# Three MoE-and-dense layers on one core: single tokens' units spread through the mixed steps, narrowing at fixed places, remainders moved

## The chip, the cores and the metric

The kernel runs on one core of a Trainium2 chip. The metric is the device time of one execution in microseconds (us); the median of three runs is compared. TensorE (PE, with its weight loads PEld), VectorE (DVE), ScalarE (ACT), GpSimd (POOL) and SyncE (SP, which here only issues DMAs) each run their own instructions in order and wait for one another by semaphores.

## The reference, cut to what matters

```python
attn = softmax(mask(scale * q @ k.T)) @ v             # 4 batches x 8 heads x 576 tokens
x = attn as 2304 tokens x 512
P = sinkhorn(exp(x @ w_gate))                          # 2304 x 8, eight rounds
out = sum over e of P[:, e] * (relu(x @ w1[e]) @ w2[e])    # 8 experts, 512 -> 1024 -> 512
r = relu(out @ w_in); result = (r * r) @ w_out         # 512 -> 2048 -> 512
```

All in float32; `w_in` and `w_out` arrive as 64-bit floats.

## The kernel before, in words

After the attention (up to about 98 us) the two layers run as 80 *steps*. Each step takes 256 hidden columns, that is one first product and one second product. Steps 0 to 31 do the MoE layer for tokens 0 to 1023 (the *pair*, two halves of 512) and for 256 *single* tokens (1024 to 1279). Steps 32 to 63 do it again for tokens 1280 to 2303, without singles. Steps 64 to 71 and 72 to 79 do the dense layer for the same two groups.

The products of a pair use seven instead of eight block products. Every operand stands as a rounded part and a remainder (`hi`, `lo`), so a block product takes three matmuls per 128 rows. ACT makes a rounded part, DVE the remainder (source minus rounded part). `store` keeps finished weights in DRAM for steps 32 to 63.

A step is a list of *units* on PE, counted from 0. A unit of the pair, or one of the two single units `w0` and `w1` of the second product, is six 512-column matmuls; `us`, the single tokens' first product, is 24 matmuls of 256 columns. `run(u)` runs a unit and then whatever was registered for this place by `after(k, f)`, "k units from now", which becomes the order on ACT, DVE, POOL and SP. Functions registered earlier stand first.

- **Steps 3 to 19 and 65 to 70 ("plain").** Eighteen units: u1 to u4 (0 to 3); a second-product unit ahead of each of u5 (5), u6 (7) and u7 (9); five more (10 to 14); w0, w1, us. In step 20 all of the second product stands ahead of u1. Each second-product unit takes one of three PSUM banks (`mm`) in turn, and DVE adds it to the accumulator (L841 or L845) before the bank is used again.
- **Steps 21 to 31 ("mixed with singles").** The second product too uses seven products (`l2_mixed`, v1 to v7), accumulated by two L925 each. All eight banks are dealt out, and the single units share one (`spare`). `out_mixed` makes four blocks r1, r3, r4, r2; `mix` (L702) combines them with four subtractions on POOL into `t1` to `t4`; ACT rounds them (L670) and DVE makes their remainders (L673). They are used by v5 (t1), v6 (t2), v7 (t3) and v4 (t4) of the next step.
- **Steps 33 to 63 and 73 to 79** are mixed without singles: 14 units.

`prep_w` makes the next weights in the same step: sums on POOL (L190 to L195), rounding on ACT (L172), remainders `blkl`, `suml`, `w2l`, `mixl` on DVE (L176), all at fixed places `at`.

*Narrowing* turns `w_in` and `w_out` into float32 in 32 pieces of 128x512. `narrow` has four parts for a piece: a 512 KB load into an `xb` buffer (SP, L282); first pass (DVE, L289 and L293); second pass (L297, L300); third pass (L304, L307, L311) and a 256 KB store to `w32` (SP, L312). `narrow_on` does the next part, and `done` counts them. In steps 3 to 19 it is called behind units 3, 6, 9 and 12, and once more right after a store, so that the next load follows it at once. By this rule three of every four pieces have their first pass three units behind their load. `settled` finishes a piece that is under way at steps 30, 62 and 70. Steps 52 to 61 and 65 to 68 call it by the table `stages`.

Of the kernel before, what the change touches and what calls it, by code (L numbers as in the profile page):

```python
# [49 lines left out]
def tile_kernel(ctx: ExitStack, tc: tile.TileContext, a):  # L50
# [113 lines left out]
    def prep_w(i, layers=(1, 2)):  # L164
# [21 lines left out]
        elif 1 in layers and n < len(steps):  # L186
# [18 lines left out]
                    load_w(2 * NS1 if n + 1 == NS1 else n + 1, 0)  # L205
                keep("blk")

            at = (4, 5, 6, 8) if n == NS1 else (2, 5, 10, 14) if n < NS1 else (2, 5, 8, 11)
            spread = n > first[2] + 1
            if spread:  # L210
                at = (6, 7, 14, 16)
# [15 lines left out]
        elif i >= 0:  # L227
# [20 lines left out]
                tt(out=r[:, 1, 0], in0=r[:, 1, 0], in1=r[:, 0, 0], op=ALU.subtract)  # L248

            if TURN <= i < NS1:  # L250
                at = (7, 8, 9, 9, 13, 15)
            elif moe:
                at = (0, 0, 0, 1, 9, 11) if i == 0 else (8, 10, 11, 12, 16, 17) if i == 1 else (1, 3, 6, 7, 13, 15)
            else:
                at = (11, 13, 14, 14, 20, 22) if late else (14, 15, 16, 16, 21, 22) if n == first[2] + 2 else (12, 13, 14, 14, 19, 20)
# [395 lines left out]
    def l1_pair(i):  # L651
# [24 lines left out]
        def out_mixed(fc, t, src, k):  # L676
# [18 lines left out]
            if (fc, t) == (0, 0):  # L695
                operand("11", g, k + 1, k + 2)
            elif (fc, t) == (1, 1):
                operand("22", g, *((5, 6) if i + 1 in first else (3, 4)))
            elif (fc, t) == (1, 0):
                operand("21", g, k + 1, k + 2 if moe else k + 3)  # L700
            else:
                sub = lambda o, x, y: nc.gpsimd.tensor_tensor(out=o, in0=x, in1=y, op=ALU.subtract)  # L702

                def mix():
                    sub(r1, r4, r1)
                    sub(r5, r2, r1)
                    sub(r4, r2, r4)
                    sub(r3, r3, r5)

                after(2, mix)  # L710
                operand("t1", r1, 3, 4)
                operand("t2", r5, 4, 5)
                operand("t3", r4, 5, 7)
                operand("t4", r3, 6, 8)

        def out(fc, t, src, k):
            if mixed(i):
# [232 lines left out]
    with tc.manual_schedule():  # L950
# [231 lines left out]
        for i in range(len(steps) + 1):  # L1182
# [23 lines left out]
            if mixed(i - 1):  # L1206
# [9 lines left out]
                    names = "u1 v1 u2 v2 u3 u4 v6 u5 v5 u6 u7 v7 v3 v4"  # L1216
                else:
                    names = "u1 v1 u2 v2 u3 v6 u4 v5 u5 v7 u6 v3 u7 v4"
                if l1s and i < NS1:
                    names += " w0 w1 us"  # L1220
                order = [(u | v)[n] for n in names.split()]
                l2, l2s, l1s, ahead = [], [], [], []
            elif i == TURN:
# [19 lines left out]
            if i == NS1 + 4:  # L1243
                y0 = two(xb()) + two(xb())
                raw = two(raw1.rearrange("p b c -> p (b c)").bitcast(F32R))
                splits.append(blocks_of(1, y_dram[:, :, :2 * T], y0 + raw))
            if i == 2 * NS1 + 1:
                y1 = two(mix32) + tuple(post[0].tile([128, T], F32, tag="pp", name="pp", bufs=3) for _ in range(2))
                splits.append(blocks_of(2, y_dram[:, :, PAIRS[1]:], y1 + two(mixes[0][0]) + two(xb().bitcast(F32R))))
                apart[:] = xb(), post[0].tile([128, T], F32, tag="pp", name="pp", bufs=3)  # L1250
            if SCALED <= i < TURN - 1:
                split_on(0, 8, 9)
            elif NS1 + 4 <= i < 2 * NS1 - 4:
# [6 lines left out]
                    after(8 + 2 * k, f)  # L1260
            stages = {}
            if 2 * NS1 - 12 <= i <= 2 * NS1 - 3:
                stages = ({8: 3, 9: 0}, {8: 1}, {8: 2})[(i - 2 * NS1 + 12) % 3]
            elif 2 * NS1 < i <= 2 * NS1 + 4:
                stages = {1: 0, 4: 1, 9: 2, 17: 3}
            early = (2, 15, 16, 17) if i == SCALED - 1 else (3, 6, 9, 12) if SCALED <= i < TURN else ()
            for k, u in enumerate(order):
                run(u)
                if i < SCALED:
                    next(sink, None)  # L1270
                if stages and done[0] % 4 == stages.get(k):
                    narrow_on()
                if k in early:
                    narrow_on()
                    if done[0] % 4 == 0:
                        narrow_on()
        settle()

# [85 lines left out]
```

## Time and profile before

| | us |
|---|---|
| median of 3 runs | 2034.26 (2031.69 to 2038.37) |
| the profiled execution | 2036.71 |
| its span, first to last instruction | 2034.9 |
| PE busy | 1922.1 (94%) |
| DVE busy | 1676.5 (82%) |
| ACT, POOL busy | 793.0 (39%), 684.8 (34%) |
| mean granted TensorE clock | 0.985 of 2.4 GHz |

A sum made from the trace is compared with the profiled execution's 2036.71. Matmul ends are modelled in the trace, so that "busy" for PE is near, not at, its peak; its idle times and the starts of its matmuls are what to read.

### The profile page before, as it was taken

The numbers are of one execution on the slowest core, as the hardware profiler recorded it, in microseconds if no ns is written. First come the engines' busy times: TensorE is split into PE (matmuls) and PEld (weight loads), VectorE is DVE, ScalarE is ACT, GpSimd is POOL, SyncE is SP. The second block draws the span as 40 slices with busy tenths as digits, with TensorE's granted clock in tenths as the row PEclk, the third lists the DMA queues.
The fourth block names the chain that finished last, engine by engine and source line by source line (L and its number), as shares of the span: only waits on it lengthen the run. The fifth ranks groups of instructions, "written<-read, shape, count | busy, mean of one in ns | idle before, by whom it ended". The sixth has DMA issues, their size and how long they took to land.

```text
span 2034.9 us, 28281 instructions
## 1 busy us (share of the span) xinstructions
PE 1922.1 (94%) x10343; PEld 1576.3 (77%) x10343; DVE 1676.5 (82%) x2468; ACT 793.0 (39%) x1310; POOL 684.8 (34%) x584
## 2 busy tenths in 40 slices
PE   8998899898999899999999999999999999999999
PEld 6677777687777777777788888888888777788887
DVE  7786777676767689999968998998999989985797
ACT  6743232232233344343433333333333344452543
POOL 3523233132132155555513423433323244240331
PEclk9999999898999999999999999999999999999999
DMA  8675676575666545564796766766666687779762
GB/s 299 237 266 208 207 251 219 207 258 191 238 224 237 188 180 182 184 217 180 274 387 244 268 245 262 268 247 255 246 230 237 248 326 279 258 275 383 267 230 80
DMA packets 162554, 492.75 MB, mean 242 GB/s; under 512 B 16928, under 2 KB 32176, under 8 KB 162416
## 3 DMA queue, kind: packets, MB, share of 16 engines
q1 hardware_dynamic: 162416, 490.96, 66.2%
q8 instruction: 81, 1.33, 0.3%
q14 instruction: 57, 0.47, 0.1%
HBM read 282.15 MB, written 208.74 MB: 241 GB/s over the span
## 4 chain that ended last, share of the span: by engine, by line
PE 68%; DVE 20%; DMA 6%; issue 2%; ACT 2%; POOL 1%; SPq 0%; DVEq 0%; POOLq 0%; ACTq 0%
PE pt L591 12%; PE mm L815 12%; PE mm L911 12%; PE s L591 9%; PE xt L591 7%; PE mm L772 5%; DMA xb<-in_w_out 4%; PE xt L911 4%; PE s L911 4%; DVE acc L925 3%; DVE acc L841 2%; DVE g L673 2%; DMA xb<-in_w_in 2%; DVE suml L176 1%; DVE s L751 1%
## 5 line engine op out<-in xcount | busy, mean ns | idle before, releaser
L815 PE MATMUL mm<-w2h,g 128*128 128x512 f32 x928 | 300.0, 405 | 38.5 <-DVE acc L841 38.1
L702 POOL TENSOR_TENSOR r<-mix,r 128x512 f32<-128x512 f32 x51 | 67.2, 1318 | 575.9 <-DVE mix L691 480.1
L673 DVE TENSOR_TENSOR g<-r,g 128x512 fp32r<-128x512 f32 x204 | 207.1, 1019 | 46.7 <-ACT g L670 45.0
L815 PEld LDWEIGHTS mm<-w2h,g 128*128 128x128 f32 x928 | 177.8, 195 | 82.6 <-DVE acc L841 44.8
L670 ACT CAST g<-r 128x512 fp32r<-128x512 f32 x204 | 126.6, 621 | 240.5 <-PE mm L911 113.6
L925 DVE TENSOR_TENSOR acc<-mm,acc 128x512 f32<-128x512 f32 x298 | 191.7, 681 | 12.8 <-PE mm L911 12.8
L815 PE MATMUL mm<-w2l,g 128*128 128x512 f32 x464 | 185.8, 400 | 0.0
L841 DVE SCALAR_TENSOR_TENSOR acc<-mm,ptile,acc 128x512 f32<-128x512 f32 x194 | 141.1, 745 | 38.9 <-PE mm L815 38.6
L190 POOL TENSOR_TENSOR sums<-raw 128x256 f32<-128x256 f32 x40 | 37.0, 924 | 370.3 <-DVE suml L176 322.9
L815 PE MATMUL mm<-w2h,sg 128*128 128x512 f32 x320 | 106.5, 415 | 32.5 <-DVE acc L841 29.1
L670 ACT CAST g<-mix 128x512 fp32r<-128x512 f32 x153 | 94.8, 620 | 86.4 <-POOL mix L702 76.9
L772 PE MATMUL mm<-xs,blkh 128*128 128x256 f32 x624 | 116.5, 287 | 12.2 <-DVE acc L841 10.2
L911 PE MATMUL mm<-g,w2h 128*128 128x512 f32 x408 | 126.3, 391 | 1.0 <-ACT s L915 1.0
L631 ACT ACTIVATE sg<-mm 128x512 fp32r<-128x512 f32 (+1 forms) x33 | 18.9, 573 | 275.3 <-PE mm L772 253.6
L591 PE MATMUL xt<-x_hi,sumh 128*128 128x512 f32 x316 | 123.8, 392 | 2.2 <-DVE s L742 2.2
L591 PE MATMUL pt<-x_hi,sumh 128*128 128x512 f32 x316 | 123.9, 392 | 2.0 <-ACT s L737 2.0
L911 PE MATMUL mm<-g,mixh 128*128 128x512 f32 x408 | 125.7, 389 | 0.0
L591 PE MATMUL s<-x_hi,blkh 128*128 128x512 f32 x316 | 123.5, 391 | 1.1 <-ACT pt L725 1.1
L591 PE MATMUL pt<-x_lo,sumh 128*128 128x512 f32 x316 | 123.4, 391 | 0.0
L591 PE MATMUL pt<-x_hi,suml 128*128 128x512 f32 x316 | 123.3, 390 | 0.0
L591 PE MATMUL s<-x_lo,blkh 128*128 128x512 f32 x316 | 123.1, 390 | 0.0
L591 PE MATMUL s<-x_hi,blkl 128*128 128x512 f32 x316 | 123.1, 390 | 0.0
(264 smaller groups left out, 5083.3 us busy)
## 6 DMA issues: line engine op xcount, KB each, us to landing
raw<-in_w SPq DMA_DIRECT2D x61, 512.0 KB, 4.2
blkh<-w_blkh SPq DMA_DIRECT2D x41, 512.0 KB, 3.7
blkl<-w_blkl SPq DMA_DIRECT2D x41, 512.0 KB, 4.6
sumh<-w_sumh SPq DMA_DIRECT2D x41, 512.0 KB, 5.2
suml<-w_suml SPq DMA_DIRECT2D x41, 512.0 KB, 6.1
w_blkh<-blkh SPq DMA_DIRECT2D x40, 512.0 KB, 5.1
w_blkl<-blkl SPq DMA_DIRECT2D x40, 512.0 KB, 6.1
w_sumh<-sumh SPq DMA_DIRECT2D x40, 512.0 KB, 5.6
```

Source lines behind the costliest of these rows:

```text
L176: nc.vector.tensor_tensor(out=w[1], in0=src, in1=w[0].bitcast(F32), op=ALU.subtract)
L190: tt(out=c(sums, 0), in0=c(raw1, 2), in1=c(raw1, 3), op=ALU.add)
L591: nc.tensor.matmul(ps, w[:, c], z[:, x, j], start=start and k == 0, stop=stop and k == 5, skip_group_check=True)
L670: after(k, lambda: nc.scalar.copy(b[:, 0], src))
L673: lambda: nc.vector.tensor_tensor(out=b[:, 1], in0=src, in1=b[:, 0].bitcast(F32), op=ALU.subtract),
L702: sub = lambda o, x, y: nc.gpsimd.tensor_tensor(out=o, in0=x, in1=y, op=ALU.subtract)
L751: after(0, lambda: nc.vector.tensor_tensor(out=made["s2"], in0=bank_c, in1=made["s2"], op=ALU.add))
L772: nc.tensor.matmul(ps, w[:, c], z[:, kc], start=k == 0, stop=k == len(terms) - 1)
L815: nc.tensor.matmul(ps, g[:, c0 * 128:c0 * 128 + 128], wt[:, fc], start=k == 0, stop=k == 3 * FC - 1)
L841: nc.vector.scalar_tensor_tensor(out=dst, in0=ps, scalar=p, in1=dst, op0=ALU.mult, op1=ALU.add)
L911: nc.tensor.matmul(ps, w[wt][:, c], z[:, g], start=start and k == 0, stop=stop and k == 2, skip_group_check=True)
L925: nc.vector.tensor_tensor(out=o, in0=ps, in1=o, op=ALU.add)
```

## The change

It does five things. In steps 21 to 31 w0, w1 and us no longer stand together at the end: w0 stands behind v2, w1 behind v6 (in step 31 too), us stays last. In steps 20 to 31 the remainders of t1 to t4 are registered later: 7, 6, 9 and 11 units behind u7 instead of 4, 5, 7 and 8; `suml` goes from place 14 to 12 in steps 21 to 30 and the rounding of `mix` from 13 to 14. In steps 3 to 19 the narrowing is called at places that depend on the step's remainder by three, so that every first pass but that of step 3 stands seven units behind its load; the last piece's third pass goes from step 30 to step 20. Step 61 starts no piece any more, so that nothing is left to settle at step 62. The five last pieces, one more than before, are narrowed in steps 64 to 69, each loaded behind unit 8 and narrowed behind units 2, 4 and 6 of the next step.

```diff
-            at = (4, 5, 6, 8) if n == NS1 else (2, 5, 10, 14) if n < NS1 else (2, 5, 8, 11)
+            at = (4, 5, 6, 8) if n == NS1 else (2, 5, 10, 12) if TURN + 1 < n < NS1 else (2, 5, 10, 14) if n < NS1 else (2, 5, 8, 11)
...
             if TURN <= i < NS1:
-                at = (7, 8, 9, 9, 13, 15)
+                at = (7, 8, 9, 9, 14, 15)
...
-                operand("t1", r1, 3, 4)
-                operand("t2", r5, 4, 5)
-                operand("t3", r4, 5, 7)
-                operand("t4", r3, 6, 8)
+                a, b, c, d = (4, 5, 7, 8) if i >= NS1 else (7, 6, 9, 11)
+                operand("t1", r1, 3, a)
+                operand("t2", r5, 4, b)
+                operand("t3", r4, 5, c)
+                operand("t4", r3, 6, d)
...
-                if l1s and i < NS1:
-                    names += " w0 w1 us"
+                if i == first[1] - 1:
+                    names = "u1 v1 u2 v2 w0 u3 u4 v6 w1 u5 v5 u6 u7 v7 v3 v4 us"
+                elif i < NS1:
+                    names = "u1 v1 u2 v2 w0 u3 v6 w1 u4 v5 u5 v7 u6 v3 u7 v4 us"
...
+            if i == 2 * NS1:
+                apart[:] = xb(), post[0].tile([128, T], F32, tag="pp", name="pp", bufs=3)
             if i == 2 * NS1 + 1:
...
-                apart[:] = xb(), post[0].tile([128, T], F32, tag="pp", name="pp", bufs=3)
...
-                stages = ({8: 3, 9: 0}, {8: 1}, {8: 2})[(i - 2 * NS1 + 12) % 3]
-            elif 2 * NS1 < i <= 2 * NS1 + 4:
-                stages = {1: 0, 4: 1, 9: 2, 17: 3}
-            early = (2, 15, 16, 17) if i == SCALED - 1 else (3, 6, 9, 12) if SCALED <= i < TURN else ()
+                stages = ({8: 3, 9: 0} if i < 2 * NS1 - 3 else {8: 3}, {8: 1}, {8: 2})[(i - 2 * NS1 + 12) % 3]
+            elif 2 * NS1 <= i <= 2 * NS1 + 5:
+                stages = {2: 1, 4: 2, 6: 3, 8: 0}
+            early = ()
+            if i == SCALED - 1:
+                early = (2, 15, 16, 17)
+            elif SCALED <= i <= TURN:
+                early = ((1, 3, 5, 12), (1, 3, 10, 12), (1, 8, 10, 12) if i < TURN else (1,))[i % 3]
...
-                    if done[0] % 4 == 0:
+                    if done[0] % 4 == 0 and i < TURN:
                         narrow_on()
```

The change adds no instruction; it moves them. Three places show it. In the changed kernel the lines from 711 on have other numbers: L841 is L842, L742 is L743, L751 is L752, L925 is L926.

First, DVE in the middle of step 13 (remainder 1): before, with the third pass of a piece, whose end releases the next load, close ahead of the next first pass.

```order
L304 TENSOR_SCALAR xb<-xb 128x512
L307 SCALAR_TENSOR_TENSOR xb<-xb 128x512
L311 TENSOR_TENSOR xb<-xb 128x512
L841 SCALAR_TENSOR_TENSOR acc_1873<-mm,ptile,acc_1873 128x4x128
L624 SCALAR_TENSOR_TENSOR g_1876<-s_152,g_1876 128x512
L624 SCALAR_TENSOR_TENSOR g_1876<-pt,g_1876 128x512
L329 TENSOR_TENSOR pp<-z_1887,pp 128x512
L751 TENSOR_TENSOR s_151<-xt,s_151 128x512
L289 TENSOR_SCALAR xb<-xb 128x512
L293 SCALAR_TENSOR_TENSOR xb<-xb 128x512
```

The same stretch of step 13 on DVE now.

```order
L176 TENSOR_TENSOR blkl_142<-raw_111,blkh_141 128x1024
L842 SCALAR_TENSOR_TENSOR acc_1873<-mm,ptile,acc_1873 128x4x128
L743 TENSOR_TENSOR s_152<-xt,s_152 128x512
L842 SCALAR_TENSOR_TENSOR acc_1873<-mm,ptile,acc_1873 128x4x128
L624 SCALAR_TENSOR_TENSOR g_1876<-s_152,g_1876 128x512
L624 SCALAR_TENSOR_TENSOR g_1876<-pt,g_1876 128x512
L329 TENSOR_TENSOR pp<-z_1887,pp 128x512
L752 TENSOR_TENSOR s_151<-xt,s_151 128x512
L842 SCALAR_TENSOR_TENSOR acc_1873<-mm,ptile,acc_1873 128x4x128
L289 TENSOR_SCALAR xb<-xb 128x512
L293 SCALAR_TENSOR_TENSOR xb<-xb 128x512
```

The third pass has gone ahead of `blkl` to unit 3, and the first pass stands one unit further back, behind unit 10.

Second, SP's queue in step 12 (remainder 0): before, the narrowing's store and load (L312, L282) stand behind the second raw weights' load and the two stores of `pp`.

```order
L158 DMA raw_111<-in_w 128x1024
L139 DMA w_blkh<-blkh_147 128x1024
L139 DMA w_blkl<-blkl_148 128x1024
L158 DMA raw_113<-in_w 128x1024
L331 DMA b_dram_99<-pp 128x512 x2
L312 DMA w_96<-xb 128x512
L282 DMA xb<-in_w_out 128x1024
L139 DMA w_sumh<-sumh_149 128x1024
```

The same place of SP's queue now.

```order
L158 DMA raw_111<-in_w 128x1024
L139 DMA w_blkh<-blkh_147 128x1024
L139 DMA w_blkl<-blkl_148 128x1024
L312 DMA w_96<-xb 128x512
L282 DMA xb<-in_w_out 128x1024
L158 DMA raw_113<-in_w 128x1024
L331 DMA b_dram_99<-pp 128x512 x2
L139 DMA w_sumh<-sumh_149 128x1024
```

The pair of L312 and L282 now follows the two `blk` stores at once, and the second raw load waits behind it.

Third, DVE at the change from one mixed step to the next: before, with the singles' accumulations of w0 and w1 (L841) around `suml`, then `mixl` and the remainders of t1 and t2 (`g<-r`).

```order
L925 TENSOR_TENSOR acc_1873<-xt,acc_1873 128x512
L841 SCALAR_TENSOR_TENSOR acc_1874<-mm,ptile,acc_1874 128x512
L176 TENSOR_TENSOR suml_144<-sums,sumh_143 128x1024
L841 SCALAR_TENSOR_TENSOR acc_1874<-mm,ptile,acc_1874 128x512
L176 TENSOR_TENSOR mixl_1881<-raw_113,mixh_1880 128x1024
L673 TENSOR_TENSOR g_1875<-r_6184,g_1875 128x512
L673 TENSOR_TENSOR g_1876<-r_6186,g_1876 128x512
L624 SCALAR_TENSOR_TENSOR sg<-mm,sg 128x512
L673 TENSOR_TENSOR g_1876<-mix_1878,g_1876 128x512 x2
L925 TENSOR_TENSOR acc_1873<-mm,acc_1873 128x512 x2
```

DVE from the end of a mixed step into the next one now.

```order
L926 TENSOR_TENSOR acc_1873<-xt,acc_1873 128x512
L624 SCALAR_TENSOR_TENSOR sg<-mm,sg 128x512
L673 TENSOR_TENSOR g_1876<-r_6190,g_1876 128x512
L926 TENSOR_TENSOR acc_1873<-mm,acc_1873 128x512 x2
L842 SCALAR_TENSOR_TENSOR acc_1874<-mm,ptile,acc_1874 128x512
L673 TENSOR_TENSOR g_1875<-r_6188,g_1875 128x512
L176 TENSOR_TENSOR blkl_142<-raw_111,blkh_141 128x1024
L691 SCALAR_TENSOR_TENSOR r_6188<-s,pp 128x512
L673 TENSOR_TENSOR g_1876<-mix_1878,g_1876 128x512
L926 TENSOR_TENSOR acc_1873<-s,acc_1873 128x512
L926 TENSOR_TENSOR acc_1873<-xt,acc_1873 128x512
L842 SCALAR_TENSOR_TENSOR acc_1874<-mm,ptile,acc_1874 128x512
```

`suml` and `mixl` have gone ahead into the step, nothing but `sg` stands between the last accumulation and the remainder of t2, and w0 and w1 are accumulated four and seven units into the next step.

## Rows read from the trace of the kernel before

**Rows 1.** The page: the span.
```profile
span 2034.9 us, 28281 instructions
```

**Rows 2.** Stretches: length; busy PE, PEld, DVE, ACT, POOL; granted clock; DMA share; GB/s.
```profile
159.42:194.14 34.72, 29.54 (x129) 24.09 (x127) 23.33 (x35) 15.07 (x22) 6.57 (x8) 0.90 0.65 219
194.14:651.77 457.63, 412.39 (x1893) 339.45 (x1892) 331.78 (x469) 134.59 (x194) 116.33 (x127) 0.96 0.63 224
...
715.15:745.10 29.95, 26.46 (x122) 21.50 (x121) 27.52 (x35) 12.40 (x19) 20.73 (x18) 0.94 0.35 127
745.10:993.40 248.30, 226.35 (x1082) 186.09 (x1081) 230.63 (x291) 100.77 (x153) 131.88 (x108) 1.00 0.55 196
...
1067.00:1600.20 533.20, 533.20 (x2353) 441.59 (x2353) 484.99 (x734) 199.65 (x352) 177.91 (x120) 1.00 0.68 251
1600.20:1624.97 24.77, 21.01 (x85) 16.82 (x84) 22.88 (x34) 7.89 (x13) 5.79 (x4) 0.93 0.56 215
...
1667.90:1780.70 112.80, 107.30 (x506) 87.05 (x505) 103.27 (x138) 52.73 (x82) 44.22 (x40) 1.00 0.78 279
1780.70:1832.70 52.00, 52.00 (x255) 44.03 (x254) 44.89 (x62) 26.69 (x41) 23.09 (x21) 1.00 0.76 278
```

**Rows 3.** PE's waits, 159.4 to 700.8: total us, times, longest.
```profile
PE mm L815 <- DVE acc L841: 49.2, 21, 4.6
```

**Rows 4.** DVE's waits in the same stretch.
```profile
DVE xb L289 <- DMA xb<-in_w_out: 45.5, 12, 4.7
...
DVE xb L289 <- DMA xb<-in_w_in: 13.3, 5, 3.4
```

**Rows 5.** Chain that ended last, step 10: start, time from issue to landing.
```profile
391.88 7.21 DMA xb<-in_w_out
```

**Rows 6.** Timeline of DVE, steps 10 and 11 (start, duration; the idle time before).
```profile
399.21 0.43 DVE L289 TENSOR_SCALAR xb<-xb 128x512 int32<-128x512 int32 x1 [4.66 <-DMA xb<-in_w_out]
...
425.42 0.43 DVE L289 TENSOR_SCALAR xb<-xb 128x512 int32<-128x512 int32 x1 [2.17 <-DMA xb<-in_w_in]
...
426.50 0.74 DVE L841 SCALAR_TENSOR_TENSOR acc<-mm,ptile,acc 128x512 f32<-128x512 f32 x1
...
432.59 0.42 DVE L304 TENSOR_SCALAR xb<-xb 128x512 int32<-128x512 int32 x1
...
434.39 1.40 DVE L841 SCALAR_TENSOR_TENSOR acc<-mm,ptile,acc 128x512 f32<-128x512 f32 x2
435.71 1.22 DVE L176 TENSOR_TENSOR suml<-sums,sumh 128x1024 fp32r<-128x1024 f32 x1
```

**Rows 7.** Timeline of PE in step 10.
```profile
401.08 1.22 PE L815 MATMUL mm<-w2h,g 128*128 128x512 f32 x2 [4.61 <-DVE acc L841]
```

**Rows 8.** PE's waits, 715.2 to 1029.1 (steps 21 to 31).
```profile
PE mm L815 <- DVE acc L841: 18.0, 11, 2.6
PE mm L772 <- DVE acc L841: 10.2, 11, 1.0
```

**Rows 9.** Groups by line, steps 22 to 30: count, busy us, mean ns, idle before.
```profile
L673 DVE TENSOR_TENSOR g<-r,g 128x512 fp32r<-128x512 f32 x36 | 38.7, 1089 | 0.0
...
L176 DVE TENSOR_TENSOR suml<-sums,sumh 128x1024 fp32r<-128x1024 f32 x9 | 18.2, 2018 | 0.0
...
L176 DVE TENSOR_TENSOR mixl<-raw,mixh 128x1024 fp32r<-128x1024 f32 x9 | 14.6, 1626 | 0.0
...
L702 POOL TENSOR_TENSOR mix<-r,mix 128x512 f32<-128x512 f32 x9 | 20.3, 2253 | 0.0
L702 POOL TENSOR_TENSOR r<-r,r 128x512 f32<-128x512 f32 x9 | 11.6, 1289 | 0.7
```

**Rows 10.** Timeline of DVE, then of PE, in step 62.
```profile
1603.21 1.66 DVE L293 SCALAR_TENSOR_TENSOR xb<-xb 128x512 int32<-128x512 int32 x1
...
1609.84 1.29 DVE L673 TENSOR_TENSOR g<-r,g 128x512 fp32r<-128x512 f32 x2
...
1611.18 0.50 PE L911 MATMUL s<-g,mixh 128*128 128x512 f32 x1 [3.76 <-DVE g L673]
```

## The prediction

> **What bounds the kernel now.** I first read the stretches [rows 2], because they compare equal work. Steps 69 and 70 do the 126 matmuls of a plain step without a PE gap, 52.00 us for two, so a plain step needs 26.0. Steps 34 to 61 are 28 steps of 14 units in 533.2 us: 1.36 a unit, 19.04 a step. A mixed step with singles has one unit less than a plain one, so it needs 26.0 - 1.36 = 24.64. Against these, steps 4 to 18 take 457.63 for 15 x 26.0 = 390, an excess of 67.6 or 4.5 a step; step 3 has 8.7; steps 22 to 30 take 248.3 for 221.8, an excess of 26.5 or 2.9 a step; step 21 has 5.3; step 62, which needs 19.04, has 5.7; steps 65 to 68 together 8.8. The rest of the program shows no such excess. So PE is the bound with gaps in it, and the question is who makes the gaps.
>
> In steps 3 to 19 PE waits for a PSUM bank that DVE has not emptied, 49.2 us in 21 waits [rows 3]. DVE is not short of time there: 331.78 busy of 457.63 [rows 2]. It waits for the narrowing's loads, 45.5 + 13.3 = 58.8 us in 17 waits [rows 4]. Step 10 shows the chain: the load takes 7.21 us [rows 5], DVE stands 4.66 us in front of the first pass, and PE stands 4.61 us in front of the next unit [rows 6, 7]. The gap has a second price. The granted clock of steps 4 to 18 is 0.96, and 0.90 in step 3, against 1.00 without gaps [rows 2]; behind a long gap matmuls run at the lower of the two clock levels for a while. That is why an excess of 4.5 a step stands beside gaps that are shorter.
>
> In steps 21 to 31 PE waits 18.0 + 10.2 = 28.2 us in 22 waits, two a step: w1 for the accumulation of w0, us for that of w1 [rows 8], because the three share one bank. DVE is nearly the bound there too: 230.63 busy of 248.3, 25.6 a step [rows 2], more than PE's 24.64. Part of that is stretched: `suml` takes 2.02 us beside POOL's subtractions, `mixl` 1.63, `g<-r` 1.09 [rows 9], where `suml` takes 1.22 elsewhere [rows 6]. POOL is stretched as well, 2.25 against 1.29 for the same subtraction [rows 9].
>
> **Steps 4 to 19.** At the excess of 4.5 a step these 16 steps lose 72.1. The new places put seven units between a load and its first pass: 7 x 1.36 = 9.5 us, against three units, 4.1, for the worst case of step 10. DVE's own delay changes this lead. In steps of remainder 1 the third pass is over soon behind unit 3 and the first pass stands behind unit 10, so the lead is near 8.5, and landings are at most 7.2 [rows 5]. In remainder 0 the load now stands right behind the two `blk` stores. DVE empties unit 4's bank, makes `blkl` (1.2) and does the third pass (432.59 to 434.39, 1.8) [rows 6], so the load is issued about 2.6 behind unit 5; the first pass gets its turn 1.5 behind unit 12: lead 8.4. Landing is estimated as 7.2 to 8.6 (7.2 and one unit more of queue), a wait of 0 to 0.5, of which the three banks hide most. In remainder 2 both leads are long, but DVE is crowded. From the end of unit 8 to the start of w1 there are seven units, 9.5 us. DVE has in that time ten ordinary instructions at 0.65 (two accumulations take 434.39 to 435.71), two passes of 1.08 (425.42 to 426.50) and the third pass of 1.8 [rows 6]: 6.5 + 2.2 + 1.8 = 10.5. So w1 waits about 1.0 for the bank of the fourth unit before it; with some slow clock, 1.4. What stays is 5 x 1.4 in remainder 2 (steps 5, 8, 11, 14, 17), 5 x 0.5 in remainder 0, and 1 for the six others: 10.5. Gain 61.6. Bounds: at worst half of the 72 stays, at best 2 does: 36 to 70.
>
> **Step 3** keeps its 8.7. Its first pass moves from behind unit 3 to behind unit 1, but its load was issued at the end of step 2. DVE now stands in front of it with `w2l`, a remainder and the accumulation of the first second-product unit queued behind it, and ACT's copy for u6 waits for that accumulation; this gap grows by some 3 us, and the one of the step's second piece goes. I take 0, bounds -3 to +3. The third pass that moves from step 30 to behind unit 1 of step 20 lies beside a second product whose units are 1.8 apart for their transposes; I take 0 for it, and at most 1 us.
>
> **Steps 21 to 31.** The excess is 26.5 for 22 to 30, 5.3 for step 21, and an estimated 3.8 for step 31 (2.6, one step's share of the 28.2 [rows 8], and slow clock behind it): 35.6. Now w1 stands three units behind w0, so DVE has two units, 2.7 us, to empty the bank; us stands nine behind w1. In DVE's new order only `sg` and the remainder of t2 stand ahead of the two L925 of v2 and of w0's accumulation, so its lag there is about 1.3. POOL's four subtractions start behind r4, at the end of the step, when PE runs us and u1 to u2 and DVE has almost nothing; `suml` and `mixl` are over by then. Without the stretching DVE has 0.8 less on `suml`, 0.4 on `mixl`, and up to 4 x 0.4 on `g<-r`: 25.6 - 2.8 = 22.8, below PE's 24.64. ACT must round t2 behind POOL's second subtraction, 2.6 us behind its start, and v6 needs t2 only seven units later. I keep 3 us for step 21's backlog from step 20 and for the change of pass. Gain 32.6. Bounds: 8, if DVE stays the bound, to 35.6.
>
> The page "SBUF — State Buffer" of the Trainium skill (section "SBUF: two separate sides") says that DVE instructions with two SBUF inputs and GpSimd exclude each other: whichever starts first holds the shared ports for its whole instruction. By it every remainder that meets POOL would wait for a whole subtraction (1.29); the four that can (t2, t1, `blkl`, t3) would cost up to 5.2, and 22.8 + 5.2 = 28.0 a step would leave no gain in these steps, 1967 in all. The rows show less on DVE's side (0.8 for `suml`), with POOL slower as well.
>
> **Steps 61 and 62.** No load at 61, so `settled` finds nothing. Today three passes run in a row at the start of step 62, L293 alone 1.66, and the remainder that v6 needs is late at 1609.84; PE stands 3.76 [rows 10]. All 5.7 come back; the bounds are 4 and 6.
>
> **Steps 64 to 69.** Five pieces instead of four, one in each of 65 to 69. DVE is busy 103.27 of 112.8 in 65 to 68 and 44.89 of 52.0 in 69 and 70 without a piece [rows 2]: with one (1.08 + 1.08 + 1.8 = 4.0) step 69 needs some 26.4 of 26.0. The waits for loads go, because the new lead is the rest of the step, but DVE stays full and one more step has a piece. I take 0, from 5 lost to 6 gained.
>
> **Sum.** 61.6 + 0 + 32.6 + 5.7 + 0 = 99.9. The profiled execution took 2036.7 (span 2034.9 [rows 1] and 1.8 around it): 1936.8. It stood 2.45 above the median of the runs, so the median forecast is **1934**, own range 1920 to 1950.
>
> **Rivals.** *The loads stay late in steps 4 to 19.* SP issues in order, and in remainder 0 the load queues behind 1.5 MB that has just been issued. If landing takes 11 us, waits of 2 to 3 come back in most steps: gain 36 instead of 62, time 1960. Against it: nothing in the rows lands in over 7.2. *DVE stays the bound of the mixed steps*, because the stretching moves with POOL: at 25.6 and some waits the gain is 8 to 16, time 1955. For it: POOL's sums (L190 to L195) follow the subtractions and now meet `blkl`. *The passes stretch everywhere.* In step 62 six of the seven instructions take 1603.21 to 1609.84, 6.6 us, where a piece takes 4.0. If every piece of steps 4 to 19 did so, 21 pieces in 16 steps would add 1.3 x 3.3 = 4.3 to DVE's 22, and it would be full: gain of about 20 there, time 1975. Against it: POOL is busy only 116 of 457 us [rows 2]. *Everything comes back*, step 3 too: 1915. *Slower:* the second raw load now waits on SP behind the narrowing's load in remainder 0. If it landed so late that `w2h`, and in DVE's order all behind `w2l`, stood, every such step would stop. It is issued some 16 us before its use and would have to take over 22 us in five steps and about 12 us longer in all 16 to eat the 100; it decides from there. That the moves change nothing would need the waits [rows 4] to be no cause of the gaps.
>
> **Chances.** Forecast 0.60; loads late 0.14; mixed steps DVE-bound 0.13; stretched passes 0.05; all back 0.05; slower 0.02; no change 0.01. A measurement of this kernel tells about 0.3% (6 us) from no change: faster 0.97, same 0.01, slower 0.02. The range 1915 to 1966 takes in the forecast's bounds and the first two rivals.
>
> **What would show it.** Right: steps 4, 7, 10 at 26.0 to 26.3 without a DVE wait for `xb`; steps 5, 8, 11 with one wait of w1 near 1.0; step 3 still near 35; steps 22 to 30 at 24.6 to 25, `suml` at 1.22, POOL's L702 near 1.3; step 62 at 19.04. Wrong: DVE waits for `xb` that stay over 1 us, a wait of PE for L673, u5 or u6 waiting for ACT in steps 21 to 31, or step 69 and 70 with new gaps over 2 us.

## The result and the profile after

The changed kernel takes **1938.96 us** (median of 4 runs, 1937.08 to 1941.28); beside it the kernel before took 2032.98 (2031.69 to 2038.37). The ratio is 0.953, 95% interval 0.951 to 0.956: faster by 94 us. The profiled execution took 1940.36 (span 1938.6), 96.35 less than that of before. The forecast was 1934, range 1915 to 1966.

The stretches of the changed kernel's trace (columns as in [rows 2]) are steps 3, 4 to 18, 21, 22 to 30, 34 to 61, 62, 65 to 68, 69 and 70:

```profile
161.70:193.98 32.28, 27.62 (x128) 22.91 (x127) 23.44 (x35) 15.07 (x22) 5.82 (x7) 0.95 0.67 228
193.98:591.50 397.52, 393.43 (x1892) 328.73 (x1891) 347.23 (x469) 134.59 (x194) 128.74 (x128) 1.00 0.72 259
...
649.25:674.03 24.78, 24.78 (x122) 20.78 (x121) 20.81 (x30) 11.00 (x17) 10.83 (x12) 1.00 0.41 152
674.03:905.05 231.02, 224.25 (x1082) 187.16 (x1081) 206.58 (x289) 99.93 (x153) 104.97 (x108) 1.00 0.59 210
976.30:1509.40 533.10, 533.10 (x2354) 441.57 (x2353) 484.95 (x734) 199.43 (x352) 177.86 (x120) 1.00 0.68 253
1509.40:1528.45 19.05, 19.05 (x85) 15.76 (x84) 17.04 (x27) 7.89 (x13) 6.00 (x4) 1.00 0.64 252
1572.50:1683.10 110.60, 106.86 (x505) 87.08 (x504) 103.50 (x140) 52.84 (x82) 42.60 (x40) 1.00 0.79 293
1683.10:1736.30 53.20, 52.68 (x254) 43.80 (x253) 46.19 (x66) 26.63 (x41) 20.52 (x21) 1.00 0.75 272
```

Beside [rows 2], stretch by stretch: steps 4 to 18 are 60.1 shorter, at a granted clock of 1.00 instead of 0.96, and DVE's busy time did not fall (347 against 332). Step 3 is 2.4 shorter, step 21 5.2, steps 22 to 30 17.3, step 62 5.7. Steps 65 to 68 gain 2.2 and steps 69 and 70 lose 1.2. Steps 34 to 61, of which the change touches only a load in the last, agree to 0.1 us.

The waits that are left in steps 3 to 19 (total us, times, longest), against [rows 3] and [rows 4]:

```profile
DVE xb L289 <- DMA xb<-in_w_out: 5.1, 5, 1.2
...
PE pt L591 <- ACT s L742: 4.7, 1, 4.7
DVE xb L289 <- DMA xb<-in_w_in: 4.6, 1, 4.6
...
PE mm L816 <- DVE acc L842: 4.0, 8, 0.7
```

PE stood 49.2 us for a bank before and stands 4.0 now; DVE stood 58.8 for loads and stands 9.7. Of these, 4.6 are step 3's (its load is older than the new places), and 5.1 are the five loads of remainder 0.

The same for steps 21 to 31, against [rows 8]:

```profile
PE mm L912 <- ACT s L916: 7.5, 10, 0.8
...
PE mm L816 <- DVE sg L624: 1.3, 1, 1.3
```

The 28.2 us of w1 and us are gone. A new wait has come, 0.8 in nearly every step: v2 (L912) for ACT's copy of v1's banks (L916). And the groups of steps 22 to 30 that answer to [rows 9]:

```profile
L673 DVE TENSOR_TENSOR g<-r,g 128x512 fp32r<-128x512 f32 x36 | 28.1, 782 | 14.7 <-ACT g L670 14.7
...
L176 DVE TENSOR_TENSOR blkl<-raw,blkh 128x1024 fp32r<-128x1024 f32 x9 | 15.9, 1765 | 0.0
...
L176 DVE TENSOR_TENSOR suml<-sums,sumh 128x1024 fp32r<-128x1024 f32 x9 | 12.9, 1434 | 0.0
...
L702 POOL TENSOR_TENSOR mix<-r,mix 128x512 f32<-128x512 f32 x9 | 11.5, 1273 | 0.0
...
L176 DVE TENSOR_TENSOR mixl<-raw,mixh 128x1024 fp32r<-128x1024 f32 x9 | 10.9, 1207 | 0.0
```

`suml` fell from 2.02 to 1.43 and `mixl` from 1.63 to 1.21, as POOL's subtractions no longer run beside them (`suml` still starts beside the end of POOL's L248, and so stays above the 1.22 that it takes alone and that the prediction named); `blkl`, which now stands beside POOL's sums, takes 1.77 instead of the 1.22 that such an instruction takes alone. DVE's busy time in these nine steps fell from 230.6 to 206.6.

The new wait, in the timeline of one of these steps (start, duration; the idle time before):

```profile
776.92 0.68 DVE L691 SCALAR_TENSOR_TENSOR mix<-s,pp 128x512 f32<-128x512 f32 x1
...
777.68 1.30 POOL L702 TENSOR_TENSOR r<-mix,r 128x512 f32<-128x512 f32 x1 [7.10 <-DVE mix L691]
...
779.02 0.62 ACT L670 CAST g<-r 128x512 fp32r<-128x512 f32 x1 [1.67 <-POOL r L702]
779.06 1.29 POOL L702 TENSOR_TENSOR r<-r,r 128x512 f32<-128x512 f32 x1
...
779.55 0.58 ACT L726 COPY pt<-s 128x512 f32<-128x512 f32 x1
...
780.13 0.39 PE L591 MATMUL xt<-x_lo,sumh 128*128 128x512 f32 x1
...
780.36 0.39 PE L591 MATMUL xt<-x_hi,suml 128*128 128x512 f32 x1
780.39 0.62 ACT L670 CAST g<-r 128x512 fp32r<-128x512 f32 x1 [0.27 <-POOL r L702]
...
780.91 0.58 ACT L916 COPY s<-mm 128x512 f32<-128x512 f32 x1
...
781.55 0.73 PE L912 MATMUL mm<-g,w2h 128*128 128x512 f32 x2 [0.80 <-ACT s L916]
```

ACT rounds t1 at 779.02 and t2 at 780.39, each as soon as POOL's subtraction is done, and takes the copy that v2 waits for only behind both. POOL starts when r4 (L691, 776.92) is there. The 0.80 counts from the modelled end of the matmul before. By the starts, which are what to read, v2 begins 1.19 behind that matmul (780.36 to 781.55), where the two before it are 0.23 apart: 0.96 us lost.

### The profile page after: what moved, and what is told of

It reads as the page before. It is cut to its first block, busy times and chain, and to the rows that moved or that the text cites. A ratio compares the mean times of both kernels' runs of the same rounds, so it can differ in the third digit from the quotient of the medians.

```text
span 1938.6 us, 28282 instructions
## 1 busy us (share of the span) xinstructions
PE 1893.0 (98%) x10343; PEld 1561.4 (81%) x10343; DVE 1663.1 (86%) x2468; ACT 791.5 (41%) x1310; POOL 660.6 (34%) x584
## 3 DMA queue, kind: packets, MB, share of 16 engines
q8 instruction: 81, 1.33, 0.3%
## 4 chain that ended last, share of the span: by engine, by line
PE 46%; DVE 8%; issue 1%; POOL 1%; ACT 0%; DVEq 0%; ACTq 0%; POOLq 0%
PE mm L912 11%; PE pt L591 9%; PE s L591 6%; PE xt L591 6%; PE mm L816 5%; PE s L912 4%; PE xt L912 4%; DVE acc L926 1%; PE mm L773 1%; DVE g L673 1%; POOL r L702 1%; DVE g L642 1%; DVE acc L846 0%; DVE mixl L176 0%; DVE mix L691 0%
## 5 line engine op out<-in xcount | busy, mean ns | idle before, releaser
L816 PE MATMUL mm<-w2h,g 128*128 128x512 f32 x928 | 289.1, 393 | 1.9 <-DVE acc L846 1.1
L673 DVE TENSOR_TENSOR g<-r,g 128x512 fp32r<-128x512 f32 x204 | 197.6, 970 | 63.2 <-ACT g L670 61.5
L816 PEld LDWEIGHTS mm<-w2h,g 128*128 128x128 f32 x928 | 172.1, 188 | 40.9 <-DVE acc L846 4.7
L926 DVE TENSOR_TENSOR acc<-mm,acc 128x512 f32<-128x512 f32 x298 | 191.4, 679 | 8.1 <-PE mm L912 8.1
L842 DVE SCALAR_TENSOR_TENSOR acc<-mm,ptile,acc 128x512 f32<-128x512 f32 x194 | 142.4, 745 | 45.8 <-PE mm L816 45.5
L816 PE MATMUL mm<-w2l,g 128*128 128x512 f32 x464 | 180.8, 390 | 0.0
L912 PE MATMUL mm<-g,w2h 128*128 128x512 f32 x408 | 127.3, 393 | 9.7 <-ACT s L916 9.7
L190 POOL TENSOR_TENSOR sums<-raw 128x256 f32<-128x256 f32 x40 | 31.3, 782 | 295.2 <-DVE suml L176 213.9
L912 PE MATMUL mm<-g,mixh 128*128 128x512 f32 x408 | 125.7, 389 | 0.0
L591 PE MATMUL xt<-x_hi,suml 128*128 128x512 f32 x316 | 123.0, 389 | 0.0
L591 PE MATMUL xt<-x_lo,sumh 128*128 128x512 f32 x316 | 123.0, 389 | 0.0
```

The lines of the kernel that those rows point to most:

```text
L190: tt(out=c(sums, 0), in0=c(raw1, 2), in1=c(raw1, 3), op=ALU.add)
L591: nc.tensor.matmul(ps, w[:, c], z[:, x, j], start=start and k == 0, stop=stop and k == 5, skip_group_check=True)
L673: lambda: nc.vector.tensor_tensor(out=b[:, 1], in0=src, in1=b[:, 0].bitcast(F32), op=ALU.subtract),
L816: nc.tensor.matmul(ps, g[:, c0 * 128:c0 * 128 + 128], wt[:, fc], start=k == 0, stop=k == 3 * FC - 1)
L842: nc.vector.scalar_tensor_tensor(out=dst, in0=ps, scalar=p, in1=dst, op0=ALU.mult, op1=ALU.add)
L912: nc.tensor.matmul(ps, w[wt][:, c], z[:, g], start=start and k == 0, stop=stop and k == 2, skip_group_check=True)
```

## The experiments

### The narrowing in steps 3 to 19

**Its old places alone.** Only the places of the passes and loads go back:

```diff
-                early = ((1, 3, 5, 12), (1, 3, 10, 12), (1, 8, 10, 12) if i < TURN else (1,))[i % 3]
+                early = (3, 6, 9, 12) if i < TURN else (1,)
```

> The changed kernel with only the places of the narrowing in steps 3 to 19 as they were (behind units 3, 6, 9, 12, load right behind a third pass); the order of the mixed steps, the remainders and steps 61 to 69 stay changed. Theory, that this part is worth what the two traces differ by in steps 3 to 19 (2.4 + 65.8): 2007, from 2000 to 2013, with DVE's waits for the loads back at some 59 us and PE's waits for DVE's accumulation near 49. Rival, that part of the 68 comes from the other edits: under 1995.

Measured: 2004.96 us (2002.63 to 2006.89), ratio to the kernel before 0.985 (0.983 to 0.987); 66.0 more than the changed kernel. DVE's waits for loads are back at 46.5 + 13.2, PE's for the accumulation at 49.7. The theory holds, and this part does not depend on the others by more than a few us.

**The lead alone.** All passes stay behind the units where the change has them; only the loads come later. A store of one column (0.06 us on DVE) in front of each load keeps SP from issuing it earlier.

```diff
+        if late:
+            nc.vector.memset(z[:, :1], 0.0)
-                early = ((1, 3, 5, 12), (1, 3, 10, 12), (1, 8, 10, 12) if i < TURN else (1,))[i % 3]
+                early = ((1, 3, 5, 9, 12), (1, 3, 7, 10, 12), (1, 5, 8, 10, 12, 16) if i < TURN else (1,))[i % 3]
-                    if done[0] % 4 == 0 and i < TURN:
+                    if done[0] % 4 == 0 and i < SCALED:
```

> The changed kernel with all its passes behind the same units, but each load of the narrowing in steps 3 to 19 three units ahead of its first pass instead of seven; a store of one column by DVE in front of the load keeps it from being issued earlier. No load then stands right behind the two stores of blk, so landings should be 4.7 to 6.0 us, against a lead of 3 x 1.36 = 4.1 less DVE's own delay. Theory (the lead makes the gain): DVE waits 1 to 2 us in most of 21 loads, the banks hide about half, so steps 4 to 19 lose 10 to 25 us: 1949 to 1964. Rival (what counts is that the passes stand apart from the accumulations of the single tokens' units, not the lead): within 3 us of the changed kernel, 1936 to 1942.

With a lead of two units the loads stand at 10, 8, 6 and 17 instead of 9, 7, 5 and 16:

> As the kernel with a lead of three units, with a lead of two (2.7 us). Theory: DVE waits 2.3 to 3.5 us per load, of which PE sees 1.5 to 2.5: 21 x 2.0 = 42 and some slow clock, 1975 to 1995. Rival (the places count, not the lead): 1936 to 1945. If the step from three units to two costs more than 1.36 us a load, the clock has a share in it.

Measured: 2004.24 us (2002.59 to 2007.47) with three units, 2010.49 (2009.89 to 2012.39) with two. The theory's direction holds and the rival falls: with the new places and the old lead nothing of the 66 us is left. Both sizes were wrong. The first loss is 65 instead of 10 to 25, the second step 6 instead of 20 to 30. The trace of the kernel with three units says why: the stretch of steps 4 to 18, DVE's waits for loads in steps 3 to 19, and one load's issue with its time to landing:

```profile
198.00:651.80 453.80, 408.97 (x1892) 336.71 (x1891) 340.25 (x489) 134.58 (x194) 119.63 (x127) 0.97 0.61 226
```

```profile
DVE xb L292 <- DMA xb<-in_w_in: 40.6, 11, 4.6
...
DVE xb L292 <- DMA xb<-in_w_out: 37.3, 12, 4.7
```

```profile
xb<-in_w_in SPq DMA_DIRECT2D x1, 512.0 KB, 8.1
```

In remainder 2 the load's place behind unit 5 is that of the two `blk` stores, and it went to the queue right behind a raw load and these two stores: 8.1 us to land (7.3 to 8.1 in the five such steps, and 7.3 to 7.7 in those of remainder 1), not the 4.7 to 6.0 that I had put down. So this kernel has a shorter lead and later landings at once, and the 65 us are not the price of the lead alone. A lead counted in units is of no use before the queue in front of the load is counted too. With two units the loads stand elsewhere, and those of remainder 1 land in 5.3 to 6.4, so part of what the shorter lead costs came back.

### The order of steps 20 to 31

**The order of the single tokens' units without the new places of the remainders:**

```diff
-                a, b, c, d = (4, 5, 7, 8) if i >= NS1 else (7, 6, 9, 11)
+                a, b, c, d = 4, 5, 7, 8
```

> The changed kernel with the four remainders of steps 20 to 31 at their old places (4, 5, 7, 8 units behind u7), the new order of the single tokens' units kept. Theory (the waits of w1 and us for the one bank were the loss, and the order takes them away): 1937 to 1946, without a wait of w1 or us for DVE. Rival (the remainders' places bring it, since DVE otherwise stands in front of t1 while POOL works): steps 21 to 31 fall back by 12 to 25 us, 1951 to 1964.

Measured: 1939.35 us (1938.41 to 1941.13), the changed kernel's time. Steps 22 to 30 of it, with DVE's busy time:

```profile
673.10:903.00 229.90, 220.18 (x289) 1.00 0.59 211
```

So the new places of the remainders bring nothing. The whole gain of these steps comes from the order of w0, w1 and us, together with the new places of `suml` and of `mix`'s rounding, which this kernel keeps; the order without these two was not run.

**The old order with everything else new.** In this kernel the remainder of t1 of step 20 is made after the next step has overwritten r1, so the second products of step 20 work with another t1; no instruction is left out.

```diff
-                if i == first[1] - 1:
-                    names = "u1 v1 u2 v2 w0 u3 u4 v6 w1 u5 v5 u6 u7 v7 v3 v4 us"
-                elif i < NS1:
-                    names = "u1 v1 u2 v2 w0 u3 v6 w1 u4 v5 u5 v7 u6 v3 u7 v4 us"
+                if l1s and i < NS1:
+                    names += " w0 w1 us"
```

> The changed kernel with w0, w1 and us one behind the other at the end of the steps up to 31, as before the change, and the remainders at their new places. Theory (the order makes the gain): w1 waits 1.5 for w0's accumulation and us 0.9 for w1's, POOL meets suml and mixl again, steps 21 to 31 lose 20 to 25 us: 1958 to 1965. Rival (the remainders' places make the gain): 1937 to 1946.

Measured: 1995.32 us (1990.13 to 1997.11): far beyond the theory's own range. Steps 22 to 30 take 276.1, more than the 248.3 before the change, at a granted clock of 0.91, and w1 waits 2.63 in the step shown below:

```profile
679.30:955.40 276.10, 244.79 (x1081) 200.37 (x1081) 198.71 (x288) 100.66 (x153) 110.64 (x108) 0.91 0.50 176
```

Two more kernels separate the edits in it. The first undoes the whole part (order, remainders, and the places of `suml`, 14, and `mixh`, 13):

> The changed kernel with the whole part on steps 20 to 31 as it was: w0, w1, us at the end, the four remainders at their old places, sumh's remainder and mixh too. The narrowing of steps 3 to 20 and of 52 to 69 stays changed. Theory (the parts add up, since each acts in steps of its own): 1939 + 25 = 1964 (1960 to 1968), steps 22 to 30 at 27.6, w1 waiting 1.6 a step. Rival (the parts depend on each other through stores and loads that share one queue): outside of 1958 to 1970.

The second adds to that only the new places of the remainders, from step 21 on:

```diff
-                a, b, c, d = 4, 5, 7, 8
+                a, b, c, d = (7, 6, 9, 11) if TURN < i < NS1 else (4, 5, 7, 8)
```

> As the kernel with the mixed part undone, but with the four remainders of steps 21 to 31 at their new places (7, 6, 9 and 11 units behind u7); step 20's stay at the old ones. Theory (with w0, w1, us at the end, remainders that move from the start of the step, where DVE stands idle, to its middle push suml and the accumulation of w0 back; w1 waits 2.6 a step, though suml is no longer stretched): steps 22 to 30 at 30 to 31, 1985 to 1998. Rival (what made those 30 us in the earlier kernel is the other move, of sumh's remainder and mixh, and the remainders alone relieve DVE): 1950 to 1966.

Measured: 1964.44 us (1963.58 to 1969.65) and 1963.78 us (1960.97 to 1964.71). The first is the theory's number, 25.5 above the changed kernel. In the second the theory falls: moved remainders push nothing back. Its rival gave the right time for a half-wrong reason, since they relieve DVE and gain nothing either. DVE's busy time in steps 22 to 30 of the one and of the other, and the waits of the second from step 22 to 32:

```profile
684.20:933.00 248.80, 227.88 (x287) 1.00 0.54 193
```

```profile
675.20:923.80 248.60, 213.95 (x288) 1.00 0.54 195
```

```profile
PE mm L816 <- DVE acc L842: 15.4, 10, 1.9
PE mm L773 <- DVE acc L842: 9.3, 10, 0.9
```

DVE works 14 us less and the nine steps last the same, with the same waits (15.5 and 9.3 in the first). So DVE's total was no bound in these steps; the moment at which DVE comes to w0's accumulation was. What made 30 us a step in the kernel above is then among what is left between the two, `suml`, `mixh` and step 20. Its timeline of DVE and PE shows `suml`:

```profile
788.13 1.21 DVE L176 TENSOR_TENSOR suml<-sums,sumh 128x1024 fp32r<-128x1024 f32 x1
...
792.87 0.73 DVE L842 SCALAR_TENSOR_TENSOR acc<-mm,ptile,acc 128x512 f32<-128x512 f32 x1
...
793.66 0.73 PE L816 MATMUL mm<-w2h,sg 128*128 128x512 f32 x2 [2.63 <-DVE acc L842]
```

At place 12 `suml` stands ahead of w0's accumulation, at place 14 behind it: 1.21 of DVE more in front of w1, and the wait is 1.13 longer than the 1.50 of the other kernel. So place 12 looks good only with the new order. This is read from the rows; no kernel ran with that move alone.

### The new wait of v2

**t2's rounding behind v1's copies:**

```diff
-                operand("t2", r5, 4, b)
+                operand("t2", r5, 5 if i < NS1 - 1 else 4, b)
```

> The changed kernel with the rounding of t2 on ACT one unit later in steps 20 to 30, so that ACT's two copies of v1's banks stand ahead of it. Theory (v2 waits 0.79 us a step because these copies queue behind a rounding that waits for POOL): the wait of PE L912 for ACT L916 goes from steps 22 to 30, the steps come to 24.6 to 24.9, and the time falls by 9 x (25.7 - 24.7) = 9, to 1930 (1928 to 1933). Rival (the chain of r4, POOL and the remainders is late anyway and some other unit waits in place of v2): a new wait of v6 or w0 of about the same length, no change (1936 to 1941).

Measured: 1938.30 us (1937.95 to 1939.72): no change. The theory's number fails. The wait is still there, 4.8 in nine steps. The timeline of ACT and PE shows what stood in t2's place:

```profile
778.78 0.62 ACT L670 CAST g<-r 128x512 fp32r<-128x512 f32 x1 [2.25 <-POOL r L702]
...
779.30 0.58 ACT L726 COPY pt<-s 128x512 f32<-128x512 f32 x1
...
779.82 0.55 ACT L916 COPY s<-mm 128x512 f32<-128x512 f32 x1
...
780.41 0.73 PE L912 MATMUL mm<-g,w2h 128*128 128x512 f32 x2 [0.50 <-ACT s L916]
```

ACT now stood 2.25 us in front of t1's rounding, with u1's copy (L726) and v1's copies behind it. So t1 as well:

```diff
-                operand("t1", r1, 3, a)
-                operand("t2", r5, 4, b)
+                operand("t1", r1, 4 if i < NS1 - 1 else 3, a)
+                operand("t2", r5, 5 if i < NS1 - 1 else 4, b)
```

> The changed kernel with the roundings of t1 and of t2 each one unit later on ACT in steps 20 to 30. Moving t2 alone left a wait of 0.5: ACT then stood in front of t1's rounding (until 778.78 in its step) and copied v1's first bank only from 779.82. Theory (v2 waits because ACT takes these copies behind whatever rounding waits for POOL): with both behind, u1's copy goes at once and v1's first copy by 779.5, ended before v2's turn; the wait of PE L912 for ACT L916 goes from steps 22 to 30, steps of 24.6 to 24.9, 1930 (1928 to 1933). Rival (DVE's chain in front of r4 is the clock of the whole step, and taking ACT's part away leaves it): steps of 25.4 and more, 1935 to 1941.

Measured: **1930.11 us** (1929.72 to 1931.12), ratio 0.948 (0.946 to 0.950). Steps 22 to 30 take 222.20, PE without a gap:

```profile
673.10:895.30 222.20, 222.20 (x1083) 1.00 0.61 218
```

**The other end of the same chain**, an earlier r4 by a later `mixl`:

```diff
-                at = (7, 8, 9, 9, 14, 15)
+                at = (7, 8, 9, 9, 14, 16)
```

> The changed kernel with only mixl one unit later on DVE, so that r4, from which POOL makes t1 to t4, stands ahead of mixl (1.21 us) in steps 20 to 31. The roundings stay where the changed kernel has them. Theory (v2 is late because POOL starts late, and POOL because r4 stands behind mixl): POOL starts 1.2 earlier, t2 is rounded by 779.9 to 780.4 at the latest, and v2 waits 0 to 0.3: steps of 24.7 to 25.1, 1930 to 1935. Rival (mixl then meets POOL's subtractions, both are stretched, and the second subtraction ends as late as before): no change, 1936 to 1941.

Measured: 1940.73 us (1939.75 to 1940.99), no change; the wait is 0.52 instead of 0.80. The rival's mechanism is in the timeline of DVE and POOL:

```profile
748.04 1.30 POOL L702 TENSOR_TENSOR r<-mix,r 128x512 f32<-128x512 f32 x1 [5.96 <-DVE mix L691]
749.09 1.33 DVE L176 TENSOR_TENSOR mixl<-raw,mixh 128x1024 fp32r<-128x1024 f32 x1
...
749.42 2.15 POOL L702 TENSOR_TENSOR r<-r,r 128x512 f32<-128x512 f32 x1
```

POOL's second subtraction, which t2 waits for, now starts beside `mixl` and takes 2.15 instead of 1.29: 0.86 of the 1.2 is given back. What the shorter wait still saves in steps 22 to 30 (231.0 to 228.6) goes at the start of step 32, where PE waits 2.9 us for the load of `blkh`; that this load is late because `mixl` and its store are is argued from their order on SP; no run shows it.

### The narrowing in steps 52 to 69

Both lines of `stages`, and the place where `apart` is set, go back:

```diff
-                stages = ({8: 3, 9: 0} if i < 2 * NS1 - 3 else {8: 3}, {8: 1}, {8: 2})[(i - 2 * NS1 + 12) % 3]
-            elif 2 * NS1 <= i <= 2 * NS1 + 5:
-                stages = {2: 1, 4: 2, 6: 3, 8: 0}
+                stages = ({8: 3, 9: 0}, {8: 1}, {8: 2})[(i - 2 * NS1 + 12) % 3]
+            elif 2 * NS1 < i <= 2 * NS1 + 4:
+                stages = {1: 0, 4: 1, 9: 2, 17: 3}
```

> The changed kernel with the narrowing's places of steps 52 to 69 as they were: a load in step 61, three passes in a row at the start of step 62, four pieces spread behind units 1, 4, 9 and 17 of steps 65 to 68. Theory (the burst in step 62 made its gap; the fifth piece in step 69 costs about what the better places of 65 to 68 give): step 62 back from 19.07 to some 24.8, step 63 from 24.9 to 23.7, steps 65 to 69 1 us longer: 1944.5 (1942 to 1948). Rival (the fifth piece in an already full step 69 takes what step 62 gets): 1937 to 1941.

Measured: 1945.30 us (1944.56 to 1945.47), 6.3 more than the changed kernel. Step 62 takes 24.8 again, and in the timeline of DVE and PE the passes stand in front of the remainder that PE waits for:

```profile
1512.14 1.67 DVE L293 SCALAR_TENSOR_TENSOR xb<-xb 128x512 int32<-128x512 int32 x1
...
1518.78 1.29 DVE L673 TENSOR_TENSOR g<-r,g 128x512 fp32r<-128x512 f32 x2
...
1520.12 0.50 PE L912 MATMUL s<-g,mixh 128*128 128x512 f32 x1 [3.77 <-DVE g L673]
```

The theory holds.

### A version with the waits that are left

```diff
-                early = ((1, 3, 5, 12), (1, 3, 10, 12), (1, 8, 10, 12) if i < TURN else (1,))[i % 3]
+                early = ((1, 3, 4, 12), (1, 3, 10, 12), (1, 7, 9, 11) if i < TURN else (1,))[i % 3]
+                if i == SCALED:
+                    early = (3, 4, 5, 12)
-                    names = "v1 w0 v2 u1 w1 v6 v5 u2 u3 v7 u4 v3 u5 v4 u6 u7"
+                    names = "v1 v2 w0 u1 v6 w1 v5 u2 u3 v7 u4 v3 u5 v4 u6 u7"
```

with t1 and t2 rounded one unit later, as above.

> A version that goes on from the kernel with the roundings of t1 and t2 one unit later (1930). Remainder 0: third pass behind unit 4 instead of 5, so that its load stands on SP ahead of the stores of blk; it should land in 5 to 6 us instead of 8.1 to 8.8, and the 0.33 to 0.36 of PE in steps 6, 9, 12, 15, 18 go. Remainder 2: passes behind units 7, 9, 11 instead of 8, 10, 12, further from the single tokens' units; the gap of 0.65 to 0.70 of w1 in steps 5, 8, 11, 14, 17 shrinks. Step 3: passes behind units 3, 4, 5 instead of 1, 3, 5, so that the load from step 2 has landed and the gap of 4.7 goes. Step 32: w0 behind v2 and w1 behind v6, so that the wait of 1.3 for sg goes. Theory (each of these waits is what its step loses): 5 x 0.5 + 5 x 0.8 + 4.5 + 1.3 = 12 of 1930: 1918 (1914 to 1924). Rival (DVE's total of work in steps 3 to 19 sets what stays, and the waits move to another bank): 1926 to 1932.

Measured: **1920.63 us** (1919.59 to 1922.80), ratio to the kernel before 0.943 (0.942 to 0.945): the fastest of all, and within the theory's range. Step 3 and steps 4 to 18 of it:

```profile
162.00:191.80 29.80, 27.89 (x128) 23.07 (x127) 23.55 (x35) 14.60 (x22) 5.50 (x6) 0.94 0.70 235
191.80:583.10 391.30, 390.95 (x1892) 329.54 (x1891) 343.29 (x469) 134.98 (x195) 132.11 (x129) 1.00 0.73 264
```

Steps 4 to 18 are 1.3 above the 390 that they need, 6.2 less than in the changed kernel, with 343 of DVE against 347: the rival, that DVE's total sets what stays, falls. Step 3 gains 2.5, not 4.5: the wait is 1.9 instead of 4.7. The expectation took for granted that the load from step 2 has landed by then. It had not: it leaves SP at 165.68, and DVE still waits for it behind unit 3:

```profile
DVE xb L289 <- DMA xb<-in_w_in: 2.9, 1, 2.9
```

The edit of step 32 brought nothing: the wait for sg went, but PE waits 0.76 for ACT's copy there instead, and a load is 0.4 late. The load of remainder 0 in step 9, of the changed kernel and of this one, from issue to landing:

```profile
xb<-in_w_out SPq DMA_DIRECT2D x1, 512.0 KB, 8.1
```

```profile
xb<-in_w_out SPq DMA_DIRECT2D x1, 512.0 KB, 5.6
```

## Why the prediction was right, and where a term was not

The three parts, each undone by itself, cost 66.0 + 25.5 + 6.3 = 97.8, against 94.0 between the medians and 96.35 between the profiles: they add up to within 4 us, as the prediction's sum took for granted. More can't be asked of them: the kernel before, run beside each, had medians from 2029.95 to 2036.47.

**Steps 4 to 19: 61.6 forecast, 65.8 found** (60.1 in 4 to 18; step 19 ended at 700.8 before [rows 3], 49.0 long, and takes 43.35 now). What stays is 7.5 in steps 4 to 18; 10.5 were to stay in all. The pattern came nearly as worked out: steps 4, 7 and 10 at 26.0; one wait of w1 in remainder 2, 0.65 to 0.70 (0.28 in step 11), where some 1.0 was forecast; in remainder 0 one of 0.33 to 0.36 in three of the five steps. The estimate of remainder 0's landing, 7.2 to 8.6, met 8.1 to 8.8. DVE therefore waits about 1.0 for each of these five loads (5.1 in all), not 0 to 0.5, which is near the prediction's own sign of being wrong; the banks hide more than half of it. The rival of late loads needed 11 and did not come; that this was the delicate place, the kernels with the shorter lead show.

**Step 3: 0 forecast, 2.4 found.** The first gap grew from 2.4 to 4.7 and the second went, as described; the second (2.8) was worth more than I allowed. The sign "step 3 still near 35" did not come: 32.3.

**Steps 21 to 31: 32.6 forecast, 25.0 found** (5.2 + 17.3, and 2.5 in step 31, 35.7 before and 33.2 now). This is the term that was mis-sized, and the failing step is the sentence that v6 needs t2 only seven units later. I looked for who needs t2, and did not ask what stands behind its rounding on ACT. There stand v1's copies, which v2 needs at once. By the starts of PE's matmuls this costs 0.96 in the step shown, and steps 22 to 30 take 25.67 each, 0.98 more than the 24.69 without the wait (the sign was 24.6 to 25). The kernel with both roundings later gets 8.85 of this back, about the 7.6 that the term fell short. It was not t2 alone, as I first thought; t1's rounding holds the same place.

A second reason given there was wrong and cost nothing: that DVE is nearly the bound. With 14 us less work on DVE and the old order the steps are as long as before; with the new order and the old remainders DVE is busy 220 of 230 and the time is the changed kernel's. The waits of w1 and us were a matter of when DVE comes to the accumulations, not of how much it has to do.

On POOL and DVE: in `mixl`'s kernel POOL's subtraction began 0.33 us behind `mixl` and lasted 2.15; the rest of `mixl` (1.33 - 0.33 = 1.0) and its own 1.29 make 2.29, nearly that. Before the change `suml`'s 2.02 is its 1.22 and 0.8, not more than the rest of a subtraction that had begun [rows 9] (in one of these steps POOL's runs from 766.70 to 767.99 and `suml` starts at 767.05, a rest of 0.94). The rule of the page "SBUF — State Buffer" in the Trainium skill (section "SBUF: two separate sides"), that the one that starts first holds the shared ports to the end of its instruction, fits these lengths to 0.2 us; the prediction read [rows 9] as speaking against it, and that was a misreading. What did not come is the price put on it, 5.2 a step: with the new order only `blkl`, 0.55, and some remainders meet POOL, and PE waits for none of them.

**Step 62: 5.7 forecast, 5.7 found**, and its undoing gives it back. **Steps 64 to 70: 0 forecast, 1.0 found**; step 69 takes 27.2 instead of 26.4, and what steps 65 to 68 gain is somewhat more. Step 63 took 24.8 in the changed kernel's profile instead of 23.7, by a wait of L912 for ACT of 1.95. The same wait is 1.96 in the profile of the kernel with the later `mixl` and 0.8 in all others with the same code there. Why is not known: the edits that tell these kernels apart lie 30 steps and more ahead.

The pieces make the profile's difference: 65.8 + 2.4 + 25.0 + 5.7 + 1.0 = 99.9; less 1.1 in step 63, and 2.3 that the changed kernel's execution lost by the end of step 2, where nothing was changed: 96.5, against 96.35.

## What to carry to other kernels

Before an instruction that can wait is moved on an engine that works in order, list what stands behind it on that engine and who needs those results first; the user of its own result is the smaller half of the question. A load's lead has to be counted in time and from its place in the issuing queue: behind a load and two stores of 512 KB each the same load took 2.5 us more, and a lead of three units instead of seven, with later landings, gave back 65 of a gain of 66 us. A high busy share beside a wait is no proof of a bound: take work off that engine and see whether the wait gets shorter.

## What the runs showed that was not expected

- The place of a load on SP's queue sets its landing: 512 KB took 8.1 to 8.8 us right behind a raw load and the two stores of `blk`, and 5.4 to 5.8 ahead of them in steps 6 to 18 of the last version. The Trainium skill, "DMA: Bandwidth & Descriptors" (section "Queues, rings and completion order"), says that each DMA engine takes the descriptors of one issuer in the order of their ring; that agrees.
- A wait row understates what PE loses, at an unchanged granted clock of 1.00. The row of v2 says 0.80; the starts say 0.96, and the first two matmuls behind it take 0.73 instead of 0.62, so that steps 22 to 30 take 25.67 each with it and 222.20 / 9 = 24.69 without. In the kernel with the order alone the rows show 0.2 for v2 and nearly nothing elsewhere, yet its steps take 25.5: by the starts v2 loses 0.40, and u5, which waits for ACT's copy of u4's bank, 0.25. That is why this kernel is hardly faster than the changed one.
- Gaps and clock: in the kernel with only the remainders moved, w1 and us wait 1.50 and 0.94 in the step read, and the granted clock of steps 22 to 30 is 1.00; in the one with 2.63 and 0.84 it is 0.91 over the stretch, and the step is 3 us longer for gaps that are 1 us longer.
